# Scores of eight heads, not four, in float32 products straight from the loaded q and k, in the tiles of later heads

## The chip, the cores and the metric

The kernel runs on one core of a Trainium2 chip. The metric is the device time of one execution in microseconds (us). Three runs of the kernel before took 854.75, 860.27 and 860.95 us; their median is 860.27 us. The engines are named as in the profile: PE (TensorE, its matrix products), PEld (its weight loads), DVE (VectorE), ACT (ScalarE), POOL (GpSimd) and SP (SyncE, which here does nothing but issue DMAs).

## What is computed

Three layers follow each other, for 4 batches of 576 tokens: attention with 8 heads of 64 columns and a decay bias from `s`, a gated layer with weights `w_in`, `conv_w` and `w_out`, and a mixer with `U`, `V`, `w_ch1` and `w_ch2`. What the change touches is the product `q k^T` of the first layer.

```python
# attention, for each of 4 x 8 heads (S = 576 tokens, D = 64)
scores = scale * np.matmul(q, k.transpose(0, 1, 3, 2))
cum = np.cumsum(np.maximum(s, 0.0), axis=-1)
bias = -(cum[:, :, :, None] - cum[:, :, None, :])
scores = np.where(causal, -1000000000.0, scores + np.minimum(bias, 0.0))
attn = np.exp(scores - np.max(scores, axis=-1, keepdims=True))
x = np.matmul(attn / (np.sum(attn, axis=-1, keepdims=True) + 1e-09), v)
# gated layer, per token (conv: 3 taps over the tokens)
h = np.maximum(x @ w_in, 0.0)
x = (h * sigmoid(conv(h, conv_w))) @ w_out
# mixer
u = x + ((x.transpose(0, 2, 1)) @ U @ V).transpose(0, 2, 1)
out = u + np.maximum(u @ w_ch1, 0.0) @ w_ch2
```

## The kernel before

**Heads.** The 32 heads (4 batches of 8) are taken one after the other; head h is one call of `att_head(h)` (line 1328), which asks for the loads of head h+1, the scores of head h, and the transposes (`transp`) and the product with v (`av`) of head h-1. The scores of a head are four blocks of 128 queries with 128, 256, 384 and 512 keys (`scores`, tiles `sc`), and a last block of 64 queries with 576 keys, which `scores4` takes for two heads at once in two halves of 288 keys. DVE adds the mask and finds the row's smallest value (line 651), ACT takes the exponential (line 668, into the tiles `P`, or `p4` for the last block), POOL divides by the sum (line 679), PE transposes (line 793, tiles `pt`), ACT copies that out (line 353), and PE multiplies with v (line 829, `av`), which ACT copies into `x` (line 851).

**Two kinds of scores.** The list `FS` (line 28) says which heads take their scores in plain float32 products; before, heads 0 to 3. For such a head `prep4` (line 573) loads q and k of one head from DRAM into the lower 64 partitions of a tile `qkF`, and two rows of the running sum of `s` beside them; one float32 product per block then gives scores and bias. There are two such tiles, for even and for odd heads. For every other head `prep` (line 608) loads q and k of a pair of heads, POOL rounds them to the shorter type fp32r (line 619, "t" from "t" in the profile), DVE subtracts that to get the rest (line 620), and `place` (line 630) copies the parts by DMA, from SBUF to SBUF, into two tiles per head, `tB` (`qkB`) and `tA` (`qkA`), with a small copy of the sum's parts from DRAM (`r_d`). Two fp32r products per block then give the scores. `products` (line 685) issues the one or the two.

**Where the tiles lie.** Before, the `qkF` tiles, the running sum `cc`, its parts `rk` and the mask as loaded (`mraw`) are slices of a large tile `ws`, which later takes weights of the gated layer (`early`, line 411). `qkA` is a ring of two tiles, the tiles t1 and t2 of `prep` are one each, the tile of v for a pair of heads (`vr`) is one.

**Beside the heads.** The weights of the gated layer come as 64-bit numbers, 512 KB a piece, and are taken apart by ACT (line 502), DVE (lines 505 and 515), ACT (353) and POOL (365); `W1_AT` says at which head each piece is asked for, and two raw tiles hold what has landed. When the eight heads of a batch are under way, the gated layer of that batch runs between the next heads' work (`m1_in`, line 893; `m1_out`, line 935); its first steps need `x` of two heads only. The mixer follows after the last head.

**What sets the order.** Each step is handed to `Plan.op` with an engine, an estimate of its duration and what it reads and writes. `Plan.order` then goes through an imagined run: whenever an engine is free there, it takes, of the steps that could start, the one that stands first in the program. The instructions of each engine are issued in the order so found, and on the chip each engine and SP's DMA issues keep to it. A DMA that has to wait (for a tile to come free) holds back all DMAs behind it.

Of the kernel before, what the change touches and what calls it, by code (L numbers as in the profile page):

```python
# [8 lines left out]
F32 = mybir.dt.float32  # L9
F32R = mybir.dt.float32r  # L10
# [8 lines left out]
B, H, S, D = 4, 8, 576, 64  # L19
NH = B * H  # L20
# [4 lines left out]
NF1, NF2 = 8, 16  # L25
KT = DM // 128

FS = range(4)
FV = range(8)

CHUNKS = [512, 512, 512, 512, 256]
# [18 lines left out]
RINGS = dict(P=2, qk=2, th=3, vv=2, qkh=1, x=2, wf=2, xs=5, g=12, hh=3, c=3, x2=4, w64=2, mh=5, o=4, snap=2, tt=4)  # L50
# [259 lines left out]
def tile_attention_moe_mixer(  # L310
# [27 lines left out]
    def dma(nbytes, fn, r, w):  # L338
        return plan.op("SP", 640, fn, r, w, late=nbytes / 360)
# [5 lines left out]
    def pe(ns, fn, r, w):  # L345
        return plan.op("PE", ns, fn, r, w)

    def mm(n, m=128):
        return max(n / 2.4 + 3, m / 1.2)
# [31 lines left out]
    def ring(pool_, cls, count, shape, dtype, name, at={}):  # L381
        n = at[pool_, cls] = at.get((pool_, cls), -1) + 1
        return pool_.buf(f"{cls}{n % count}", shape, dtype, name)
# [15 lines left out]
    ap = Pool(plan, "ap", "right", after=[dec.opened])  # L399

    def one(pool_, name, shape, dtype):
        return pool_.buf(name, shape, dtype, name)
# [8 lines left out]
    def early(name, at, shape, dtype, rows=128):  # L411
        n = 1
        for x in shape:
            n *= x
        axes = " ".join("abc"[: len(shape)])

        def view(t):
            v = t[:rows, at : at + n]
            if dtype != F32:
                v = v.bitcast(dtype)  # L420
            return v.rearrange(f"p ({axes}) -> p {axes}", **dict(zip("abc", shape)))

        return Part(ws, view, name)
# [13 lines left out]
    sm4s = [one(ap, f"sm4_{i}", [128, 5], F32) for i in range(2)]  # L437


    cc = early("cc", 0, (S,), F32, NH)  # L440
    rk = early("rk", 4 * S, (2, S), F32R, NH)
    qkFs = [early(f"qkF_{i}", (6 + 2 * i) * S, (2, S), F32) for i in range(2)]

    def cum():
        return cc()
# [127 lines left out]
    def prep4(h):  # L573

        t = qkFs[h % 2]
        a = slice(64 * (h % 2), 64 * (h % 2) + 64)
        dma(294912, lambda: nc.sync.dma_start(out=t[64:128], in_=qk[h // 2, a]), [], [(t, "q")])
        rows = dma(
            2304, lambda: nc.sync.dma_start(out=t[0:1, 1, :], in_=cum()[h : h + 1]), [cc], [(t, "r0")]
        )  # L580
        if h < 2:
            dma_act(lambda: nc.scalar.dma_start(out=t[1:2, 0, :], in_=cum()[h : h + 1]), [cc], [(t, "r1")])
        else:
            dma(2304, lambda: nc.sync.dma_start(out=t[1:2, 0, :], in_=cum()[h : h + 1]), [cc], [(t, "r1")])
        st.setdefault("first", rows)
        st[h] = dict(qk=[t], P=p_tiles(h), sm=sms[h % 2])

    def prep_v(h):

        vr = ring(ap, "vr", 1, [128, 2, 5, 64], F32, f"vr{h}")  # L590
        dma(327680, lambda: nc.sync.dma_start(out=vr(), in_=vP[h // 2]), [], [vr])
        for o in range(2):
            if h + o in FV:
                st["v", h + o] = (vr, lambda j, o=o: vr[:, o, j, :])
                continue
            vv = ring(ap, "vv", RINGS["vv"], [128, 5, 128], F32R, f"vv{h + o}")
            hi_pool(lambda vv=vv: vv[:, :, 0:64], lambda o=o: vr[:, o], [vr], [(vv, 0)], 320)
            lo_pool(
                lambda vv=vv: vv[:, :, 64:128],
                lambda o=o: vr[:, o],  # L600
                lambda vv=vv: vv[:, :, 0:64],
                [vr, (vv, 0)],
                [(vv, 1)],
                320,
            )
            st["v", h + o] = (vv, lambda j, vv=vv: vv[:, j, :])
# [78 lines left out]
    def products(h, ps, rows, q0, k0, w):  # L685
# [11 lines left out]

        pe(16 + 1.88 * w if h in FS else 2 * mm(w, rows), mms, d["qk"], [ps])

# [606 lines left out]

    prep4(0)
    prep_v(0)
    mraw = early("mraw", 10 * S, (192,), F32)
    dma(98304, lambda: nc.sync.dma_start(out=mraw(), in_=mask_d), [], [mraw])  # L1310
    for c, n in ((0, 384), (512, 224)):
        o = pool(n, lambda c=c, n=n: nc.gpsimd.memset(mask[:, c : c + n], 0.0), [], [(mask, c)], extra=0)
# [15 lines left out]
    def att_head(h):  # L1328

        if h + 1 < NH:  # L1330
            if h % 2 == 1:
                prep_v(h + 1)
            if h + 1 in FS:
                prep4(h + 1)
# [140 lines left out]
    for g in range(2):  # L1475
        blk = (w2a, u1p)[g].buf(f"u{g}", [128, 2 * 7 * S], F32R, f"w2_{g}")
        for i in range(7):
            f = 7 * g + i
# [90 lines left out]
```

## Time and profile before

| | |
|---|---|
| median of three runs | 860.27 us (854.75 to 860.95) |
| the profiled execution | 857.56 us, of which its span 855.7 us |
| PE busy | 813.2 us, 95% of the span |
| PEld, DVE, ACT, POOL busy | 738.0, 610.0, 459.9, 365.3 us |
| DMA | 123.31 MB, 144 GB/s over the span |
| mean granted clock of PE | 0.995 of 2.4 GHz |

A stretch's rows give the busy time of each engine in it; what PE lacks to the stretch's length is PE's idle time. The granted clock is a share of 2.4 GHz: a mean below 1 says that PE ran at 1.2 GHz for a part of the stretch. In the timeline a row is one instruction, or several of one kind that follow each other, with start, duration, the number of them behind an x, and in brackets the idle time ahead of it with what ended that. Products overlap in the pipeline, so the cost of one is read from its start to the start of the next.

### The profile page before, as it was taken

How to read it: one execution, taken by the hardware profiler on the slowest of the kernel's cores; microseconds unless marked ns; L12 is line 12 of the kernel's file. 1: busy time of each engine (PE TensorE's matmuls, PEld its weight loads, DVE VectorE, ACT ScalarE, POOL GpSimd, SP SyncE). 2: the span in 40 equal slices, each digit the busy share in tenths (PEclk: the TensorE clock that was granted, in tenths of full speed). 3: DMA queues.
4: the chain of work that ended last, by engine and by line, in shares of the span. 5: the costliest groups of instructions: out<-in, count | busy, mean ns of one | idle time of the engine just before them, and what ended most of it. 6: DMA issues, size and time to landing. Idle time of an engine off the chain costs nothing. (4 is left out here: it accounts for less than half of the span.)

```text
span 855.7 us, 15636 instructions
## 1 busy us (share of the span) xinstructions
PE 813.2 (95%) x5300; PEld 738.0 (86%) x5300; DVE 610.0 (71%) x1362; ACT 459.9 (54%) x1144; POOL 365.3 (43%) x461
## 2 busy tenths in 40 slices
PE   5889899999999999999999989999999999999998
PEld 2556689889999998998999889999998888888888
DVE  6865899986997769978878998777878762323232
ACT  4776888875987668875766423223233432222211
POOL 4675777574455734457345663333344220000000
PEclk9998999999999999999999999999999999999999
DMA  6868844573455524512133336445467764545443
GB/s 198 234 161 199 202 136 121 141 188 80 122 131 146 129 58 128 149 51 82 34 115 121 118 107 204 145 144 179 138 188 235 256 203 121 163 123 165 130 123 99
DMA packets 67624, 123.31 MB, mean 144 GB/s; under 512 B 9412, under 2 KB 34884, under 8 KB 67544
## 3 DMA queue, kind: packets, MB, share of 16 engines
q1 hardware_dynamic: 67472, 122.30, 50.1%
q8 instruction: 42, 0.69, 0.3%
q14 instruction: 38, 0.31, 0.1%
q10 hardware_dynamic: 72, 0.01, 0.0%
HBM read 68.88 MB, written 28.90 MB: 114 GB/s over the span
## 5 line engine op out<-in xcount | busy, mean ns | idle before, releaser
L1270 PE MATMUL my<-mh,w 128*128 128x512 f32 (+1 forms) x560 | 158.9, 368 | 0.0
L1174 PE MATMUL ma_S<-u,W 128*128 128x288 f32 x768 | 119.2, 296 | 7.6 <-DVE s L1190 7.5
L1251 DVE SCALAR_TENSOR_TENSOR ml<-ml,mh 128x512 fp32r<-128x512 f32 (+1 forms) x80 | 51.9, 654 | 98.3 <-ACT mh L1248 98.3
L935 PE MATMUL y<-gh,w1o 128*128 128x288 f32 x512 | 118.1, 301 | 0.7 <-DVE c L914 0.4
L1270 PEld LDWEIGHTS my<-mh,w 128*128 128x128 f32 x560 | 101.6, 189 | 17.4
L1174 PEld LDWEIGHTS ma_S<-u,W 128*128 128x128 f32 x768 | 107.5, 188 | 10.2 <-DVE s L1190 10.0
L1248 ACT ACTIVATE mh<-ml 128x512 fp32r<-128x512 f32 (+1 forms) x80 | 46.9, 589 | 118.8 <-DMA ml<-ch_d 74.0
L679 POOL TENSOR_SCALAR P<-P,sm 128x128 f32<-128x128 f32 (+3 forms) x128 | 74.9, 602 | 82.2 <-DVE sm L725 61.4
L1270 PE MATMUL my<-ml,w 128*128 128x512 f32 (+1 forms) x280 | 103.0, 368 | 0.0
L1174 PE MATMUL ma_A<-u,W 128*128 128x288 f32 x576 | 92.9, 296 | 0.5 <-DVE s L1190 0.4
L935 PEld LDWEIGHTS y<-gh,w1o 128*128 128x128 f32 x512 | 86.4, 188 | 2.2 <-DVE c L914 1.1
L651 DVE CUSTOM_DVE_ANT_0 sc<-sc,mask 128x128 f32<-128x128 f32 (+2 forms) x144 | 68.8, 494 | 24.3 <-PE sc L690 17.1
L1174 PEld LDWEIGHTS ma_A<-u,W 128*128 128x128 f32 x576 | 81.8, 188 | 1.4 <-DVE s L1190 0.9
L365 POOL TENSOR_TENSOR gl<-c,gh 128x288 fp32r<-128x288 f32 x64 | 53.9, 846 | 64.3 <-ACT gh L920 60.7
L893 PE MATMUL h<-xh,w1h 128*128 128x290 f32 x256 | 80.0, 313 | 0.5 <-DVE c L914 0.5
L893 PE MATMUL h<-xl,w1h 128*128 128x290 f32 x256 | 76.4, 298 | 0.7 <-POOL xl L365 0.7
L893 PE MATMUL h<-xh,w1l 128*128 128x290 f32 x256 | 76.3, 298 | 0.0
L935 PE MATMUL y<-gl,w1o 128*128 128x288 f32 x256 | 75.1, 293 | 0.6 <-POOL gl L365 0.6
L668 ACT ACTIVATE P<-sc,sm 128x128 f32<-128x128 f32 (+3 forms) x128 | 67.5, 530 | 11.2 <-DVE sm L651 9.5
L905 DVE SCALAR_TENSOR_TENSOR c<-h,cw,c 128x288 f32<-128x288 f32 x128 | 64.3, 509 | 5.3 <-ACT c L901 4.3
L1186 ACT COPY p<-ma_A 128x288 f32<-128x288 f32 x64 | 25.5, 399 | 73.0 <-PE ma_A L1174 57.7
L362 DVE TENSOR_TENSOR tl<-pt,th 128x384 fp32r<-128x384 f32 x96 | 54.3, 566 | 12.4 <-ACT th L353 12.1
(145 smaller groups left out, 1990.6 us busy)
## 6 DMA issues: line engine op xcount, KB each, us to landing
ml<-ch_d SPq DMA_DIRECT2D x64, 256.0 KB, 2.6
ch_d<-s SPq DMA_DIRECT2D x64, 144.0 KB, 1.8
raw_w<-w_in SPq DMA_DIRECT2D x16, 512.0 KB
raw_w2a<-w_in SPq DMA_DIRECT2D x16, 512.0 KB, 4.7
raw_w2b<-w_in SPq DMA_DIRECT2D x16, 512.0 KB, 4.4
t<-qk_in SPq DMA_DIRECT2D x28, 288.0 KB, 2.9
qkA<-t SPq DMA_DIRECT2D x56, 144.0 KB, 4.0
qkA<-t SPq DMA_DIRECT2D x28, 288.0 KB, 3.0
```

The source lines that it names most:

```text
L362: dve(n, lambda: nc.vector.tensor_tensor(out(), src(), f32(hi()), ALU.subtract), r, w)
L365: pool(n, lambda: nc.gpsimd.tensor_tensor(out(), src(), f32(hi()), ALU.subtract), r, w, two=True)
L651: lambda: nc.vector.tensor_tensor_reduce(out=ps[:rows, :w], in0=ps[:rows, :w], in1=mask[:rows, m0 : m0 + w], scale=-0.125, scalar=3.0e38 i ...
L668: lambda: nc.scalar.activation(out(), ps[:rows, :w], ACTF.Exp, bias=low(), scale=-1.0, accum_out=total()),
L679: lambda: nc.gpsimd.tensor_scalar(t[:, :w], t[:, :w], r(), 1.0, ALU.mult, ALU.mult),
L893: nc.tensor.matmul(ps[:, :W], lhsT=ww, rhs=xx, start=kt + n == 0, stop=kt == KT - 1 and n == 2)
L905: lambda k=k: nc.vector.scalar_tensor_tensor(c(), hh[:, k : k + HS], cw[:, 3 * f + k : 3 * f + k + 1], c(), ALU.mult, ALU.add),
L935: nc.tensor.matmul(ps[:, :HS], lhsT=ww, rhs=xx(), start=f + n == 0, stop=f == NF1 - 1 and n == 2)
L1174: nc.tensor.matmul(ps[:, :HS], lhsT=ww, rhs=uu, start=k == 0, stop=k == 5)
L1248: act(n, lambda: nc.scalar.activation(mh[:, :n], raw(), ACTF.Relu), [ml], [mh])
L1251: lambda: nc.vector.scalar_tensor_tensor(ml[:, :n], raw(), 0.0, f32(mh[:, :n]), ALU.max, ALU.subtract),
L1270: nc.tensor.matmul(ys[c][dt][:, :n], lhsT=ww, rhs=xx[:, :n], start=f + k == 0, stop=f == NF2 - 1 and k == 2)
```

## The change

`FS` becomes heads 0 to 7. Heads 4 to 7 so take `prep4` and one float32 product per block where they took `prep`, `place` and two fp32r products. The two `qkF` tiles are now the first two of the ring `qkA`, so that the first `place` (heads 8 and 9) waits for the float32 heads to be done with them. The running sum gets a tile of its own, and `rk` and `mraw` move within `ws`.

```diff
-FS = range(4)
+FS = range(8)
...
-    cc = early("cc", 0, (S,), F32, NH)
-    rk = early("rk", 4 * S, (2, S), F32R, NH)
-    qkFs = [early(f"qkF_{i}", (6 + 2 * i) * S, (2, S), F32) for i in range(2)]
+    cc = one(ap, "cc", [NH, S], F32)
+    rk = early("rk", 0, (2, S), F32R, NH)
+    qkFs = [ring(ap, "qkA", RINGS["qk"], [128, 2, S], F32, f"qkF_{i}") for i in range(2)]
...
-    mraw = early("mraw", 10 * S, (192,), F32)
+    mraw = early("mraw", 2 * S, (192,), F32)
```

The planner finds another order for the first part of the program. PE's order is the same again, instruction for instruction, from the last product of head 16 with v on (3103 rows to the end).

SP's issues around the loads for heads 4 and 5, before: `t1`, `t2` hold a pair's parts, lines 638 are the copies of `place`, 525 weights, 618 loads of `prep`, 591 v.

```order
L638 DMA qkA4_291<-t2_4_192 64x576
L638 DMA qkA5_332<-t2_4_192 64x1152
L638 DMA qkB_0_154<-t1_4_200 64x1152
L638 DMA qkB_1_159<-t1_4_200 64x1152
L525 DMA raw_w1_4_0_353<-w1_in 128x512
L638 DMA qkA5_332<-t1_4_200 64x576
L638 DMA qkA5_332<-t2_4_192 64x576
L525 DMA raw_w1_5_0_400<-w1_in 128x512
L618 DMA t1_6_416<-qk_in 128x576
L618 DMA t2_6_423<-qk_in 128x576
L591 DMA vr2_435<-vP_in 128x640
```

And SP's issues at the same place now, where 577, 579 and 584 are the load of q and k and the two rows of `prep4` for head 4:

```order
L525 DMA raw_w1_3_0_305<-w1_in 128x512
L525 DMA raw_w1_4_0_334<-w1_in 128x512
L618 DMA t2_8_361<-qk_in 128x576
L618 DMA t1_8_366<-qk_in 128x576
L638 DMA qkB_0_157<-r_d_57 4x1152
L577 DMA qkF_0_104<-qk_in 64x1152
L579 DMA qkF_0_104<-cc_108 1x16x36
L584 DMA qkF_0_104<-cc_108 1x16x36
L525 DMA raw_w1_5_0_416<-w1_in 128x512
L591 DMA vr2_425<-vP_in 128x640
```

The copies of heads 4 and 5 are gone, one load of q and k stands for them, and the loads of heads 8 and 9 have come forward.

SP's issues ahead of the load of v for heads 4 and 5 (`vr4`), before:

```order
L525 DMA raw_w1_0_512_592<-w1_in 128x512
L638 DMA qkB_0_154<-r_d_57 4x1152
L638 DMA qkB_0_154<-t1_6_416 64x1152
L638 DMA qkA6_626<-t2_6_423 64x1152
L638 DMA qkA6_626<-t1_6_416 64x576
L591 DMA vr4_648<-vP_in 128x640
L638 DMA qkA6_626<-t2_6_423 64x576
```

and now, with head 6's load on `qkF_0`:

```order
L525 DMA raw_w1_7_0_522<-w1_in 128x512
L525 DMA raw_w1_0_512_560<-w1_in 128x512
L577 DMA qkF_0_104<-qk_in 64x1152
L579 DMA qkF_0_104<-cc_108 1x16x36
L584 DMA qkF_0_104<-cc_108 1x16x36
L525 DMA raw_w1_1_512_624<-w1_in 128x512
L591 DMA vr4_631<-vP_in 128x640
```

Around `vr4` the three copies of head 6 have become one load and two rows, and a weight piece stands among them.

PE at the first scores of head 4, before (`pt2` are transposes of head 2, `av2` its product with v):

```order
L793 MATMUL pt2_2_473<-ident_134,P2_2_336 128x128
L690 MATMUL sc4_0_482<-qkB_0_154 128x128
L690 MATMUL sc4_0_482<-qkA4_291 128x128
L690 MATMUL sc4_1_488<-qkB_0_154 128x256
L690 MATMUL sc4_1_488<-qkA4_291 128x256
L829 MATMUL av2_0_491<-tf2_0_451,vr2_435 64x256
```

and now (`h0_0_0` is the gated layer's first block):

```order
L690 MATMUL sc4_0_464<-qkF_0_104 128x128
L793 MATMUL pt2_2_469<-ident_137,p4_1_150 128x128 x2
L793 MATMUL pt2_2_469<-ident_137,P2_3_359 128x128
L793 MATMUL pt2_2_469<-ident_137,P2_2_321 128x128
L690 MATMUL sc4_1_479<-qkF_0_104 128x256
L893 MATMUL h0_0_0_482<-xh0_0_106,w1h_0_241 128x290
L893 MATMUL h0_0_0_482<-xl0_0_110,w1h_0_241 128x290
L893 MATMUL h0_0_0_482<-xh0_0_106,w1l_0_252 128x290
L829 MATMUL av2_0_490<-tf2_0_438,vr2_425 64x256
```

Each pair of products is one, the transposes stand between the two blocks, and one group of three products of the gated layer has come this far forward. In all 24 pairs become single products. Of the gated layer's groups of three, eight stand ahead of head 8's first scores before, and one now; ahead of head 10's first scores it is 16 before and 20 now.

## Rows read from the trace of the kernel before

**Rows 1.** Busy us per stretch: PE, PEld, DVE, ACT, POOL, then clock, DMA share, GB/s.
```profile
17.00:41.00 24.00, 20.82 (x101) 11.90 (x99) 20.12 (x51) 18.80 (x52) 17.64 (x20) 1.00 0.86 224
41.00:55.00 14.00, 13.44 (x75) 9.06 (x74) 12.56 (x37) 12.41 (x35) 9.34 (x13) 1.00 0.44 139
55.00:67.00 12.00, 8.90 (x48) 6.26 (x47) 4.29 (x12) 5.63 (x16) 8.55 (x9) 0.86 0.98 202
67.00:85.00 18.00, 16.00 (x86) 11.47 (x84) 10.82 (x32) 13.16 (x37) 11.37 (x14) 0.91 0.81 206
85.00:110.00 25.00, 21.39 (x134) 17.12 (x134) 22.15 (x61) 19.76 (x54) 17.07 (x22) 1.00 0.81 209
110.00:193.00 83.00, 80.35 (x591) 76.35 (x590) 74.87 (x212) 69.85 (x201) 59.20 (x89) 1.00 0.57 142
```

**Rows 2.** Timeline of PE, its three longest waits between 17 and 85 us.
```profile
38.12 0.52 PE L793 MATMUL pt<-ident,P 128*128 128x128 f32 x3 [1.57 <-ACT x L851]
...
61.45 4.58 PE L829 MATMUL av<-tf,vr 128*64 128x256 f32 x14 [2.34 <-DMA vr<-vP_in]
...
79.28 0.48 PE L793 MATMUL pt<-ident,p 128*128 128x128 f32 x1 [2.00 <-POOL p L679]
```

**Rows 3.** Timeline of PE, float32 scores of heads 2 and 3, each with its successor.
```profile
21.53 0.82 PE L690 MATMUL sc<-ws 128*128 128x128 f32 x4
22.18 0.38 PE L793 MATMUL pt<-ident,p 128*128 128x128 f32 x2
...
32.26 1.38 PE L690 MATMUL sc<-ws 128*128 128x288 f32 x4 [0.26 <-ACT P L668]
33.48 2.22 PE L829 MATMUL av<-tf,vr 128*64 128x320 f32 x10
...
39.75 1.02 PE L690 MATMUL sc<-ws 128*128 128x512 f32 x2
40.61 0.38 PE L793 MATMUL pt<-ident,p 128*128 128x128 f32 x2
```

**Rows 4.** Timeline of PE, fp32r scores of heads 4 and 6, each with its successor.
```profile
46.38 0.40 PE L690 MATMUL sc<-qkB 128*128 128x512 f32 x1
...
46.85 0.49 PE L793 MATMUL pt<-ident,P 128*128 128x128 f32 x3
...
65.96 0.33 PE L690 MATMUL sc<-qkB 128*128 128x128 f32 x1
...
66.52 0.49 PE L793 MATMUL pt<-ident,P 128*128 128x128 f32 x3
...
67.25 0.34 PE L690 MATMUL sc<-qkB 128*128 128x384 f32 x1
...
67.61 0.27 PE L793 MATMUL pt<-ident,p 128*128 128x128 f32 x1
...
71.32 0.32 PE L690 MATMUL sc<-qkB 128*128 128x288 f32 x1
...
71.87 0.29 PE L893 MATMUL h<-xh,w1h 128*128 128x290 f32 x1
```

**Rows 5.** DMA issues from 0 to 110 us: count, KB each, median us to landing.
```profile
qkA<-t SPq DMA_DIRECT2D x16, 144.0 KB, 4.2
...
ws<-qk_in SPq DMA_DIRECT2D x4, 288.0 KB, 4.6
```

**Rows 6.** Timeline of SP, the issue of `vr4`.
```profile
54.48 1.50 SPq L591 DMA_DIRECT2D vr<-vP_in  x1
```

**Rows 7.** Waits of SP's DMA queue from 8 to 110 us: total, times, longest.
```profile
SPq L618 <- DMA qkA<-t: 13.1, 6, 4.9
```

**Rows 8.** Timeline of ACT, the weight piece just ahead of head 1's copy into `x`.
```profile
36.86 0.67 ACT L502 ACTIVATE raw_w<-raw_w 128x512 f32<-128x512 f32 x1 [1.47 <-DMA raw_w<-w_in]
```

**Rows 9.** Timeline of POOL and of DVE, one rounding and one subtraction of `prep`.
```profile
69.35 0.68 POOL L356 TENSOR_SCALAR t<-t 128x576 fp32r<-128x576 f32 x1 [4.48 <-DMA t<-qk_in]
...
72.64 0.74 DVE L362 TENSOR_TENSOR t<-t,t 128x576 fp32r<-128x576 f32 x1
```

## The prediction

> **What bounds the kernel now.** I read the busy times by stretch first, then PE's timeline with its waits, then the timelines and waits of SP and ACT. PE is busy for 95% of the span, and its order is the same again from the last product of head 16 on, which the trace puts near 193 us. What the change is worth is therefore settled before 193 us: what PE gains or loses there is carried to the end, since the work behind is the same, in the same order. Four stretches from 17 to 85 us, the time from head 1 to the first scores of head 8, show PE idle for 3.18, 0.56, 3.10 and 2.00 us [rows 1], 8.8 us together. In two of them the mean granted clock is 0.86 and 0.91. A part f at 1.2 GHz makes the mean 1 - f/2, so work that full speed does in half the time stood for 0.14 x 12 = 1.7 us and 0.09 x 18 = 1.6 us more, 3.3 us together. So 12.1 us are lost there. From 85 to 110 us PE is idle for 3.6 us, from 110 to 193 us for 2.6 us [rows 1]. No other engine is full in these stretches (ACT 18.80 of 24, DVE 20.12 of 24 us), but the DMA engines are busy for 0.81 to 0.98 of three of the four [rows 1]. The reader should see a stage in which many engines wait for each other and DMA is the nearest to full.
>
> The three longest waits tell how [rows 2]. At 38.12 us PE waits 1.57 us for an ACT copy; ACT itself had waited 1.47 us for a weight piece that had not landed [rows 8]. At 61.45 us PE waits 2.34 us for the tile of v of heads 4 and 5; its issue ends at 55.98 us [rows 6], so it took 5.5 us to land among the copies of heads 6 and 7, and the following 14 records took 4.58 us, most of them at 1.2 GHz. At 79.28 us PE waits 2.00 us for POOL's division of the last block.
>
> **What is added.** 24 products in float32 take the place of 48 in fp32r. In float32 the blocks of 128 and 256 keys take 22.18 - 21.53 = 0.65 us together, the one of 512 takes 40.61 - 39.75 = 0.86 us, and two of the four halves of the last block 33.48 - 32.26 = 1.22 us [rows 3]; two halves are one head's share. The block of 384 keys has as many columns as the first two together, so I take 0.65 us. That is 3.38 us a head. In fp32r the same are 66.52 - 65.96 = 0.56, 46.85 - 46.38 = 0.47, 71.87 - 71.32 = 0.55 and, for 384 keys, 67.61 - 67.25 = 0.36 us [rows 4], together 1.94 us. The difference is 1.44 us a head, **+5.8 us** for four heads, 5.4 to 6.5 if each block is off by 0.03 us or so. PE has this work in a stage where it is 85% busy on average, so little of it hides by itself: it counts in full, and only waits that go can pay for it.
>
> **What is removed.** Per head four copies of 288, 288, 144 and 144 KB and one of 18 KB, and for two pairs the loads of 576 KB; added is one load of 288 KB a head with two rows of 2 KB. That is 4.8 MB out and 1.2 MB in, 3.6 MB less. From 17 to 85 us the rates of [rows 1] times the lengths give 13.5 MB, so a quarter of the traffic goes. SP has 12 issues fewer (20 copies and 4 loads out, 12 in), and the loads of `prep` no longer stand behind the copies of heads 4 to 7; such waits held SP's queue for 13.1 us in all from 8 to 110 us [rows 7]. POOL loses four roundings of 0.68 us and DVE four subtractions of 0.74 us [rows 9], 2.7 and 3.0 us. Neither is on PE's path by itself; they shorten queues ahead of it.
>
> Wait by wait. (a) `vr4`: its competitors, the copies of heads 6 and 7, are gone, but a load of 288 KB and a weight piece of 512 KB now stand right ahead of it. PE has, between the last reader of the old v and the first of the new, the scores 5_0 to 5_3 and 6_0 to 6_2 in float32 (2.16 + 1.30 us) and two to three groups of transposes (some 1.3 us before at 0.3 to 0.6 us each, an estimate), about 4.8 us of cover against a landing of 5.5 us with more traffic around it. I take the wait down to 0.5 us and the 1.7 us of clock behind it as gone: **-3.5** (-4.0 to 0). (b) The wait at 38.12 us: the weight piece of [rows 8] now competes with two loads rather than six copies: **-1.0** (-1.6 to 0). (c) The wait at 79.28 us rests on DVE, ACT and POOL in turn and on two weight pieces that ACT meets ahead of the last block's exponentials in the new order as well; two of DVE's subtractions stood in that chain. I leave it and its clock as they are: **0** (-3.6 to +2). (d) The rest of the idle time to 85 us is 8.8 - 5.9 = 2.9 us in short waits; a quarter less traffic and the shorter queues of POOL and DVE take a third: **-1.0** (-2 to +1). (e) Seven groups of three products of the gated layer come later than before and are there to fill PE between heads 8 and 10, where it is idle for 3.6 us: **-1.3** (-2.5 to +1).
>
> **What is new.** Heads 4 to 7 now wait, as heads 2 and 3 did, until the head two before is done with the tile. Then come three issues and a landing of 4.6 us [rows 5]. For head 4 there is much room: its tile is free when the last block of head 2 is done at 33.5 us [rows 3], and its scores start after 40 us. For head 6 the cover is the same work as in (a), about as long as the load; behind the waiting load SP holds a weight piece and `vr4`. For head 8 three copies, each 4.2 us to landing [rows 5], wait for head 6's last block, with a like cover. I take 0.3 us for each: **+0.6** (0 to +4: one of them late by 2.3 us as `vr4` was, with 1.7 us of clock). The moved tiles cost nothing else: `cc`, `rk` and `mraw` are read by the same steps as before, and the first use of `ws` by weights comes later than their last.
>
> The sum is 5.8 - 3.5 - 1.0 - 1.0 - 1.3 + 0.6 = -0.4 us, on the profiled execution's 857.6 us: 857.2 us. The median of the three runs lies 2.7 us above that execution, so the same change on it gives **859.9 us**.
>
> The clock is the least certain term. Rows show it fall around the wait of 2.34 us and in the stretch with the wait of 2.00 us, and not in the stretch with the one of 1.57 us [rows 1, 2]. The Trainium skill, TensorE: Matmul & The Clock Gate, section "What's actually happening", has the chip judge activity in windows that run free of the kernel, so that the same wait may or may not cost the clock from one kernel to the next; by that the 3.3 us could come back with shorter waits, and the sum would be 1.7 us higher, or 1.6 us lower if the second drop goes by luck. The trace neither bears this out nor speaks against it.
>
> **The rivals.** First, DMA was the real bound up to 85 us, and with a quarter of it gone PE runs through: nearly all of the 12.1 us go, and half of the 3.6 us behind. Then 5.8 - 12.1 - 1.8 = -8.1 us, 852.2 us on the median. For it speaks the DMA share of 0.81 to 0.98; against it that the wait at 79 us hangs on POOL, and that weights still come at the pace at which ACT and DVE free the raw tiles.
>
> Second, the slower one: PE's waits stay because weight pieces, not copies, are what ACT and DVE stand behind. ACT takes a piece apart ahead of the last block's exponentials of heads 4 and 6; a piece that lands late holds the exponentials, POOL's division and PE's transposes. Then nothing of (a) to (e) comes back, and the time is +5.8 us, 866.1 us on the median; with one more wait like that of `vr4`, 2.3 + 1.7 us, it is 870 us. It decides when the pieces of 512 KB land later than the about 5 us that PE's work covers.
>
> Third, the added products fall into time in which PE would wait anyway, since ACT and DVE set the pace, while copies and roundings were hidden as well. Then the price is a part of 5.8 us and the gain a part of (a): within 2 us of no change, 858 to 862 us.
>
> **How the numbers follow.** The forecast, -4 to +3 us, has a chance of 0.50; the third rival, which ends in the same place, 0.17; the first 0.13; the second 0.20. One per cent is 8.6 us, about what a measurement of this kernel can tell from no change. Faster by over 1% needs more than the first rival's 8.1 us: half of its chance, 0.06. Slower by over 1% needs the second rival with its further wait: 0.08. Within 1%: 0.86. The range reaches from the first rival's 852.2 to the second's 866.1 us, rounded outwards to 852 and 867; the likeliest case's own range is 856 to 863 us.
>
> **What would show it.** Right: the 24 float32 products of heads 4 to 7 cost what those of heads 2 and 3 did; `vr4` lands within 5 us and PE waits under 1 us for it; the clock in the stretch around it stays at 1.00; PE's idle time to head 8's first scores falls to 4 to 6 us; the last product of head 16 with v ends within 4 us of where it did, and the time from there to the end is the same. Wrong: waits of 2 us or more at head 6's or head 8's first scores, or at the transposes of the last blocks, with a fall of the clock behind them; or no waits at all there.

## Result, and the profile after

In the runs beside each other the changed kernel took 849.47 us (848.97 to 850.11), the kernel before 858.89 us; the ratio is 0.990 with a 95% interval of 0.988 to 0.992. A second set on another chip gave 850.40 us, 0.991 (0.989 to 0.993). The forecast was 859.9 us with a range of 852 to 867: the time lies 10.4 us under the forecast and below the range. Of that, 1.4 us is the kernel before itself, which stands at 858.89 us here and stood at 860.27 us when the forecast was made.

The profiled execution has a span of 847.6 us for 855.7 us, 8.1 us less. First the windows of after by stretch, the columns as in [rows 1]; the last two cut the time at head 8's first scores and at head 16's last product with v.

```profile
17.00:41.00 24.00, 22.36 (x109) 13.31 (x109) 20.00 (x55) 20.20 (x56) 19.44 (x20) 1.00 0.61 189
41.00:55.00 14.00, 13.46 (x62) 7.70 (x63) 11.32 (x25) 10.48 (x28) 8.23 (x11) 1.00 0.69 171
55.00:67.00 12.00, 10.43 (x52) 6.03 (x51) 9.78 (x26) 9.14 (x26) 8.23 (x9) 1.00 0.54 167
67.00:85.00 18.00, 16.74 (x87) 10.48 (x86) 11.45 (x37) 14.74 (x42) 11.73 (x16) 1.00 0.70 186
85.00:110.00 25.00, 24.74 (x177) 22.73 (x176) 24.14 (x65) 22.78 (x63) 20.58 (x26) 1.00 0.60 165
...
17.00:77.30 60.30, 55.30 (x261) 32.08 (x260) 49.41 (x126) 48.12 (x131) 42.84 (x47) 1.00 0.60 173
77.30:185.54 108.24, 105.92 (x770) 98.81 (x768) 95.28 (x272) 91.08 (x260) 75.65 (x114) 1.00 0.62 157
```

The kernel before, cut at the same two places of its program:

```profile
17.00:84.49 67.49, 58.65 (x299) 38.18 (x297) 47.79 (x128) 49.48 (x137) 46.80 (x54) 0.95 0.78 198
84.49:193.17 108.68, 102.42 (x729) 94.15 (x728) 97.20 (x273) 90.12 (x256) 76.37 (x111) 1.00 0.63 157
```

Three things are to be seen. PE's idle time from 17 us to head 8's first scores fell from 8.84 to 5.00 us. The clock is 1.00 there, where 0.95 over 67.49 us stood for 3.4 us. And behind that point the same part of the program takes the same time (108.24 for 108.68 us), with 3.9 us less idle time and 3.5 us more work: seven groups of the gated layer that stood ahead of head 8 now stand behind it. Their 21 products make some 3 us of that, at 0.13 to 0.14 us each from start to start (before's timeline):

```profile
87.20 0.30 PE L893 MATMUL h<-xh,w1h 128*128 128x290 f32 x1
87.33 0.30 PE L893 MATMUL h<-xl,w1h 128*128 128x290 f32 x1
```

So 7.2 of the 8.1 us are won before head 8's first scores (84.49 to 77.30 us). From head 16's last product to the end it is 662.1 us, before 662.5.

The clock is a large part of the gain, and not in these two executions alone. Over all executions on record the granted clock, averaged over the span, has a mean of 0.992 to 0.993 in the kernel before (by chip) and of 0.998 to 0.999 in the kernel after; on 858 us that is some 4 to 6 us, an estimate.

PE's timeline after, at the waits that answer to [rows 2]:

```profile
37.70 0.30 PE L793 MATMUL pt<-ident,p 128*128 128x128 f32 x1 [1.40 <-ACT P L668]
...
58.00 0.33 PE L793 MATMUL pt<-ident,p 128*128 128x128 f32 x1 [1.57 <-POOL p L679]
...
60.49 0.86 PE L829 MATMUL av<-tf,vr 128*64 128x256 f32 x4
...
76.77 0.33 PE L793 MATMUL pt<-ident,p 128*128 128x128 f32 x1 [0.31 <-POOL p L679]
...
77.30 0.31 PE L690 MATMUL sc<-qkB 128*128 128x128 f32 x1
```

The wait for `vr4` (2.34 us) is gone: the row at 60.49 us has no bracket. The wait at the last block ahead of head 8 is 0.31 us for 2.00. Two waits of 1.4 and 1.6 us are left, on ACT's exponentials and on POOL's division. SP's timeline and its waits show the load's place:

```profile
53.68 0.37 SPq L591 DMA_DIRECT2D vr<-vP_in  x1
```

```profile
SPq L618 <- DMA qkA<-t: 3.2, 3, 1.5
```

The issue took 0.37 us for 1.50 [rows 6] and began 0.8 us earlier, and the loads of `prep` stood 3.2 us behind copies for 13.1 [rows 7].

### The profile page after: what moved, and what is told of

The parts are those of the page before. It is cut to its first block, busy times and chain, and to the rows that moved or that the text cites. A ratio compares the mean times of both kernels' runs of the same rounds, so it can differ in the third digit from the quotient of the medians.

```text
span 847.6 us, 15572 instructions
## 1 busy us (share of the span) xinstructions
PE 812.5 (96%) x5300; PEld 736.3 (87%) x5300; DVE 608.0 (72%) x1358; ACT 460.3 (54%) x1144; POOL 363.0 (43%) x457
```

## The experiments

All ratios are to the kernel before on the same chip. Since the program behind head 8's first scores takes 107.9 to 109.9 us to head 16's last product in every kernel with after's order, the time of head 8's first scores tells what a change of the first part costs; "idle" is PE's from 17 us to there, "clock" the mean there. These three columns come from one profiled execution each: after and c1, the same kernel, differ by 0.2 us at head 8's first scores and by 0.7 us at head 16's last product. The medians hold more than the first part: the profiled executions of c1, e2, e3, e5 and e9 have one or two falls of the clock between 400 and 500 us, where PE's order is after's, those of after, e1, e4 and e10 none.

| kernel | median, us | ratio, 95% interval | head 8's first scores | idle | clock |
|---|---|---|---|---|---|
| before (profile above) | 858.89 | | 84.49 | 8.84 | 0.95 |
| after | 849.47 | 0.990 (0.988 to 0.992) | 77.30 | 5.00 | 1.00 |
| after again (c1) | 850.40 | 0.991 (0.989 to 0.993) | 77.06 | 5.05 | 1.00 |
| e1: copies back | 857.18 | 0.998 (0.997 to 0.999) | 83.81 | 10.26 | 0.97 |
| e2: roundings back | 852.71 | 0.992 (0.991 to 0.994) | 78.85 | 7.00 | 1.00 |
| e3: both back | 859.96 | 1.001 (1.000 to 1.003) | 86.22 | 10.54 | 0.93 |
| e4: cheap products | 850.02 | 0.989 (0.988 to 0.991) | 78.43 | 10.48 | 0.97 |
| e5: copies of 4 KB | 856.61 | 0.997 (0.994 to 0.999) | 81.16 | 7.20 | 0.97 |
| e9: 8 copies ahead of `vr4` | 854.56 | 0.996 (0.994 to 0.998) | 81.53 | 7.43 | 0.95 |
| e10: 8 copies behind it | 851.99 | 0.993 (0.991 to 0.996) | 78.78 | 7.33 | 1.00 |

**What was removed, put back: e1, e2, e3.** The kernel after gets copies like those of heads 4 to 7 back with no reader (e1; two of 288 and two of 128 KB a head, without the small copies from `r_d` and the loads of `prep`), the four roundings and four subtractions (e2), or both (e3). The order of PE, ACT and of the rest of DVE's steps stays that of after.

```diff
+    def extra(h):
+        if not 4 <= h < 8:
+            return
+        after = st[2]["pe", 0, 0] if h < 6 else st[4]["pe", 512, 288]
+        for n in range(4):
+            t = xd[4 * (h % 2) + n]
+            r, w = (128, S) if n < 2 else (64, 512)
+            o = plan.op("SP", 0, lambda t=t, r=r, w=w: nc.sync.dma_start(out=flat(t)[:r, :w], in_=flat(xsrc)[:r, :w]), [xsrc], [t])
+            o.preds.add(after)
...
+        st[h] = dict(qk=[t], P=p_tiles(h), sm=sms[h % 2])
+        extra(h)
```

> The kernel after, with copies of the same sizes as those of heads 4 to 7 issued by SP at about the places that they had (four a head, 288, 288, 128 and 128 KB, from a filled tile into tiles that are not in use yet); nothing reads them, and the order of PE, DVE and ACT is that of the kernel after. If the traffic of the copies made the waits and the falls of the clock before (theory one), this costs 6 to 9 us: 855 to 859 us, with waits of 1.5 us or more for v or for a weight piece and a clock under 1 in the stretch from 45 to 85 us. If the roundings on POOL and DVE made them (theory two), or the order of the instructions (theory three), it stays within 1.5 us of the 849.5 us of the kernel after.

> The kernel after, with four roundings of 128x576 on POOL and four subtractions on DVE put back at about the places that those of heads 4 to 7 had, on tiles that nothing reads; no DMA is added. Theory one (traffic of the copies) and theory three (order): 849 to 851 us. Theory two (queues of POOL and DVE): 853 us or more, with longer waits of PE for the division of the last blocks.

> The kernel after with the copies and the roundings put back together, in the order of the kernel after, and with its float32 products. Theories one and two: what the two single runs cost adds up, 855 to 862 us. Theory three (the order of the kernel after has fewer waits whatever else runs): 852 us or less.

e1 gives back 7.7 us, e2 3.2 us, e3 10.5 us: put back in this way, copies and roundings cost 10.5 us, nearly the sum of the parts, and e3, which has both beside after's float32 products and in after's order, is as slow as before. PE's timeline in e1, and in e3:

```profile
66.88 0.83 PE L849 MATMUL av<-tf,vr 128*64 128x256 f32 x4 [3.57 <-DMA vr<-vP_in]
```

```profile
32.55 0.33 PE L813 MATMUL pt<-ident,p 128*128 128x128 f32 x1 [3.74 <-ACT P L688]
...
68.27 1.51 PE L849 MATMUL av<-tf,vr 128*64 128x256 f32 x4 [3.66 <-DMA vr<-vP_in]
```

With the copies the wait for `vr4` is there again, larger than before. One reason is their place: before has three copies and a small one ahead of `vr4`, e1 a block of all eight, and a weight piece (SP's timeline in e1):

```profile
55.86 5.40 SPq L582 DMA_DIRECT2D xd<-xsrc  x8
...
61.99 0.38 SPq L611 DMA_DIRECT2D vr<-vP_in  x1
```

So the 7.7 and 10.5 us are the price of copies in blocks of eight; no run measures it at before's places.

With the roundings alone (e2) there is no wait for `vr4`; PE's waits from 8 to 200 us (total, times, longest), in e2 and then in after, tell what they did:

```profile
PE pt L813 <- ACT P L688: 4.0, 4, 1.3
PE pt L813 <- POOL p L699: 1.3, 2, 1.0
PE av L849 <- ACT tf L353: 0.7, 1, 0.7
```

```profile
PE pt L793 <- ACT P L668: 2.6, 3, 1.4
PE pt L793 <- POOL p L679: 1.9, 2, 1.6
```

PE waits 1.4 us longer for exponentials and 0.7 us for one of ACT's copies ahead of a product with v, and not longer for POOL's division. Together it is 2.0 us more idle time to head 8's first scores, with no single long wait and no fall of the clock up to there.

**What was added, taken out: e4.** Heads 4 to 7 take two bf16 products per block, on the upper halves of the numbers in the same tiles and in after's order; their scores are coarser.

```diff
-            for c, t in enumerate(d["qk"]):
+            two = 4 <= h < 8
+            ts = [t().bitcast(BF16).rearrange("p a (n two) -> p a n two", two=2)[:, :, :, 1] for t in d["qk"]] * 2 if two else d["qk"]
+            for c, t in enumerate(ts):
```

> The kernel after, where heads 4 to 7 take two products of one pass per block (on the upper halves of the same float32 numbers, so the scores are coarser) in place of one float32 product: PE has the product time of the kernel before there, in the order of the kernel after. If the float32 products count in full, as the prediction had it, this gives 849.5 - 5.8 = 843.7 us; if they lie in time in which PE would wait anyway, 848 to 850 us; in between, the part that counts is read off.

The time stays (850.02 for 849.47 us). The windows of e4 to head 8's first scores, and its waits from 8 to 200 us:

```profile
17.00:78.43 61.43, 50.95 (x262) 30.31 (x261) 49.00 (x127) 48.60 (x133) 42.72 (x47) 0.97 0.62 172
```

```profile
PE pt L795 <- POOL p L679: 3.4, 2, 2.3
PE pt L795 <- ACT P L668: 2.5, 2, 1.3
PE sc L692 <- ACT p L668: 1.8, 5, 0.7
```

PE is busy for 50.95 us, 4.35 us less than in after, and with the clock at 0.97 (1.8 us of the 61.43) about 6 us less work is done. The idle time grew by 5.5 us. So the added product time is as large as forecast, and nearly all of it lies in time in which PE would wait for POOL and ACT: taking it out buys nothing. The low clock has a part in this: it follows the wait of 2.3 us for POOL's division, and without its 1.8 us head 8's first scores would come at some 76.6 us, 0.7 us ahead of after's. And the order was held: a planner that knew of the shorter products might have put other work there.

**Twelve heads: e7.** `FS` becomes heads 0 to 11, for the stretch where PE is fuller.

```diff
-FS = range(8)
+FS = range(12)
```

> The kernel after with twelve heads in float32 products rather than eight. Heads 8 to 11 run where PE is busy for 97 to 99% in the kernel after. If float32 products are free only where PE waits anyway, four heads more cost up to 4 x 1.44 = 5.8 us less a little for their copies: 851 to 856 us. If the copies and roundings are dear everywhere, another 3 us or more are gained: 846 us or less.

```profile
PE 821.8 (96%) x5300; PEld 738.9 (87%) x5300; DVE 606.8 (71%) x1354; ACT 460.7 (54%) x1144; POOL 357.7 (42%) x453
```

854.59 us, 0.996 (0.994 to 0.999) of before, 5.1 us above after and 4.2 us above c1. PE's busy time on the page is 9.3 us above after's 812.5; with the mean clock of 0.996 (3.4 us of 854.0) that leaves 5.9 us for four heads' products. The low clock lies far behind them, between 400 and 500 us, so what they cost is read up to head 16's last product with v, which starts at 189.53 us in e7. Windows of e7, and of after to the same product:

```profile
17.00:189.53 172.53, 167.76 (x1024) 130.51 (x1023) 141.52 (x392) 139.71 (x388) 114.31 (x156) 1.00 0.51 137
400.00:500.00 100.00, 91.80 (x648) 88.98 (x647) 83.58 (x145) 55.53 (x124) 51.66 (x45) 0.97 0.27 91
```

```profile
17.00:185.54 168.54, 161.22 (x1027) 130.90 (x1026) 144.69 (x397) 139.21 (x390) 118.49 (x160) 1.00 0.61 163
```

At a clock of 1.00 in both, PE has 6.5 us more work and 2.6 us less idle time, and comes there 4.0 us later. The same price that cost nothing in heads 4 to 7 is mostly paid in heads 8 to 11, although copies and roundings went there as well. The planner's order is another one, so the split is not exact.

**Half of the change: e6, e8, e11.** e6 gives the kernel before a second tile of v; e8 gives it eight float32 heads and leaves the tiles where they were; e11 moves the tiles and leaves four float32 heads.

```diff
-        vr = ring(ap, "vr", 1, [128, 2, 5, 64], F32, f"vr{h}")
+        vr = ring(ap, "vr", 2, [128, 2, 5, 64], F32, f"vr{h}")
```

> The kernel before with two tiles for v, so that the load for heads 4 and 5 need not wait for heads 2 and 3 and lands early. If the wait of 2.3 us for it and the fall of the clock behind it cost what they show, this gives 859 - 4 = 855 us, with the clock at 1.00 in the stretch from 55 to 67 us. If the stage is held up by everything that shares the DMA engines, another wait takes its place: 858 us or more.

> The kernel before with eight heads in FS and nothing else: the float32 tiles stay in the tile that takes the second half of the gated layer's weights, which so has to wait until head 7's scores are done, some 25 us later than in the kernel after. If the move of the tiles matters, this loses a good part of the gain: 853 to 860 us, with raw weight tiles held and waits of ACT or PE between 50 and 110 us. If it does not: 849 to 851 us.

> The kernel after with four float32 heads, not eight: the tiles lie where the change puts them, the rest of the work is that of the kernel before, and the planner orders it anew. Theory 'the gain needs both halves of the change' (e8, the eight heads without the move of the tiles, came out at 1.003 of the kernel before): copies and roundings of heads 4 to 7 stand ahead of the load of v again, so 855 to 860 us, 0.996 to 1.002 of the kernel before. Rival 'the place of the tiles is what brings it': 849 to 852 us.

e6: 860.24 us, 1.003 (1.000 to 1.005). The wait for v is gone and another stands at the place of the first of [rows 2], larger; ACT had waited 3.78 us for a weight piece there:

```profile
39.73 0.59 PE L793 MATMUL pt<-ident,P 128*128 128x128 f32 x3 [3.90 <-ACT x L851]
```

e8: 861.29 us, 1.003 (1.001 to 1.006). Head 8's first scores come at 79.19 us, 5.3 us before the kernel before's; head 16's last product ends at 195.21 us, 2 us after it. The planner finds another order behind head 8, with the loads bunched (windows of e8, columns as in [rows 1]):

```profile
100.00:110.00 10.00, 7.45 (x46) 6.00 (x45) 7.06 (x17) 6.94 (x18) 7.52 (x12) 0.98 0.90 252
110.00:120.00 10.00, 10.00 (x69) 9.98 (x68) 8.99 (x26) 8.65 (x27) 5.18 (x8) 0.85 0.15 33
```

PE idles 2.6 us while DMA is at 0.90, and a stretch at the low clock follows. What in the old layout makes the planner choose so is not known. e11: 855.75 us, 0.998 (0.996 to 1.000); no long wait for v is left there, and POOL's divisions are waited for instead (6.6 us in seven waits from 8 to 200 us). Head 8's first scores come at 81.58 us, 2.9 us before the kernel before's, with the clock at 1.00 to there, and that is lost again behind them.

e11 says one thing more. It has the copies and roundings of heads 4 to 7, and its expectation was that they stand ahead of `vr4` again. They do not: in the planner's new order SP issues it behind one copy and the small one of head 6, and PE waits at most 0.3 us for a load of v.

```profile
52.67 0.35 SPq L591 DMA_DIRECT2D vr<-vP_in  x1
```

So a wait for `vr4` does not follow from the copies being there; where they stand in SP's queue decides with it. As to the two halves: each alone wins ahead of head 8's first scores, loses it behind and leaves the time within 0.4% of before. That only both together keep the gain is shown; why is not, since the planner's order differs in each.

**Queue or bytes: e5, c1, e9, e10.** e5 is e1 with copies of 4 KB, as many and at the same places in SP's queue. e9 puts back only the eight copies of heads 6 and 7, ahead of `vr4`; e10 puts the same eight behind it. c1 is after, once more.

```diff
-            r, w = (128, S) if n < 2 else (64, 512)
+            r, w = 16, 64
```

```diff
-        if not 4 <= h < 8:
+        if not 6 <= h < 8:
...
+        vrd = dma(327680, lambda: nc.sync.dma_start(out=vr(), in_=vP[h // 2]), [], [vr])
+        if h == 4:
+            extra(6, vrd)
+            extra(7, vrd)
```

The first hunk of the second diff alone is e9; e10 has the other lines, and `after` is then `vrd`.

> As e1_copies, with the same 16 issues by SP at the same places, but each copies 4 KB only (16 rows of 256 bytes). If the copies cost by the bytes that they put on the DMA engines, this is within 1.5 us of the kernel after: 848.5 to 851 us. If they cost by SP's time (issues, and loads queued behind them), it is near e1_copies: 854 to 858 us.

> The kernel after, once more, as the measure for the three runs beside it on the same chip. Earlier it stood at 0.990 of the kernel before; if the chip makes no difference, 0.988 to 0.992 here.

> The kernel after with eight copies of no use put back (the four of head 6 and of head 7, two of 288 KB and two of 128 KB each), issued by SP just ahead of the load of heads 4 and 5's v; TensorE, ScalarE and VectorE keep their order. Theory 'the order of the queue': the eight issues take SP 5.4 us (as in e1, 55.86 to 61.26), the load of v is issued some 6 us later and TensorE waits for it again, 2.5 to 3.5 us, with a stretch at the low clock behind it: +4 to +7 us on the kernel after. Theory 'what counts is the bytes': the 1.66 MB take some 6 to 9 us of the sixteen DMA engines wherever they stand, so this run and e10_behind8 cost alike.

> The same eight copies with the same bytes as in e9_ahead8, issued by SP behind the load of v and behind head 7's q and k (58.24 us in the kernel after), where SP has nothing to issue until 64.39 us. Theory 'the order of the queue': the eight issues of 0.67 us fit this gap, nothing is late, 0 to +1 us on the kernel after. Theory 'the bytes': the load of v is still under way (issued 53.68, used from 60.5) and the next two weight pieces are fetched beside 1.66 MB more, so a wait of 1 us or more comes back and it costs like e9_ahead8.

SP's timeline in e5, e9 and e10, in this order:

```profile
53.98 5.33 SPq L582 DMA_DIRECT2D xd<-xsrc  x8
...
60.03 0.38 SPq L611 DMA_DIRECT2D vr<-vP_in  x1
```

```profile
52.26 5.12 SPq L582 DMA_DIRECT2D xd<-xsrc  x8
...
58.18 0.57 SPq L611 DMA_DIRECT2D vr<-vP_in  x1
```

```profile
52.71 0.37 SPq L610 DMA_DIRECT2D vr<-vP_in  x1
...
57.31 6.19 SPq L582 DMA_DIRECT2D xd<-xsrc  x8
```

And PE's, in e5 and in e9, where v is first used (in e10 that row has no wait):

```profile
64.10 1.41 PE L849 MATMUL av<-tf,vr 128*64 128x256 f32 x4 [2.67 <-DMA vr<-vP_in]
```

```profile
63.22 1.51 PE L849 MATMUL av<-tf,vr 128*64 128x256 f32 x4 [3.50 <-DMA vr<-vP_in]
```

Eight issues of 4 KB take SP 5.33 us, eight of 288 and 128 KB 5.12 us: an issue of these copies costs SP some 0.65 us whatever it moves. Of e1's 6.5 us at head 8's first scores the tiny copies alone bring 3.9, of its 6.7 us at head 16's last product 5.1 (192.26 and 190.61 for 185.54 us), so SP's time is the larger part. By the medians e5 is as slow as e1, but its profiled execution loses 3.4 us at the low clock between 400 and 500 us. Whether the bytes cost something of their own is less sure. e10 was expected to cost nothing or up to 1 us by the theory of the queue. Against c1 it cost 1.6 us on the median, with intervals that overlap; in the profiled executions, of which e10's is the fastest of its six, it is 1.7 us at head 8's first scores and 0.9 us at head 16's last product (187.08 for 186.21 us). Its idle time, 7.33 us, is that of e9. What sets e9 apart is the clock, 0.95 over 64.53 us or 3.2 us, as the idle time stands in one wait of 3.50 us; in e10 it is spread over waits up to 1.8 us. The DMA engines are full in e10 from 55 to 67 us:

```profile
55.00:67.00 12.00, 10.54 (x55) 6.33 (x54) 8.67 (x26) 10.30 (x29) 5.78 (x8) 1.00 1.02 265
```

So the theory of the queue holds: the issues make `vr4` late and cost the clock behind its wait. That the bytes make everything else on the DMA engines a little late fits e10's idle time, but its cost of about 1 us is within what executions of one kernel differ by.

The Trainium skill, DMA: Bandwidth & Descriptors, section "Issuing engines are not separate DMA queues", calls the time that the sequencer takes to start a DMA usually small relative to the DMA itself. For one it is, here some 0.65 us against the 4.2 us to landing of before's copies [rows 5]; for eight in a row, 5.33 us in e5, it is not.

## Why the prediction was wrong, point by point

**The frame held.** The order of PE from head 16's last product on is unchanged and so is the time from there (662.1 for 662.5 us). Everything is decided ahead of it, as the prediction said. Of its signs of being right, PE's idle time of 4 to 6 us to head 8's first scores (5.00), the short wait for `vr4` (none) and the clock at 1.00 came true; the one that weighs the whole sum did not, since head 16's last product came 7.6 us earlier and not within 4.

Up to that product the sum can be laid beside the trace. PE's work, with the low clock taken out, rose by 3.5 us where +5.8 was entered. Idle time and low clock up to head 8's first scores fell by 7.2 us where (a) to (d) and the new waits made -4.9. Idle time behind them fell by 3.9 us where (e) had -1.3. That is -7.6 us for -0.4.

**The step that failed first: "it counts in full, and only waits that go can pay for it".** The size of +5.8 us was right: e7's busy time gives 5.9 us for four heads, e4's about 6. But e4 shows its price in time as nothing (+0.5 us without it, within the intervals). The prediction weighed the work against PE's mean share of 85% in the stage (it is 87% up to head 8's first scores, 58.65 of 67.49 us) and took idle time as something that other terms would remove; it did not ask whether the added products stand where PE waits for ACT, DVE and POOL. They do. The wait at 79.28 us, which step (c) left at 0, shows it: in after that row waits 0.31 us, e4 with the shorter products 1.13 us at the same place. The longer products ahead of it fill the time in which POOL gets to its division. The other half of it is the planner's: with eight float32 heads seven groups of the gated layer (21 products of some 0.14 us, 2.9 us) moved from ahead of head 8 to behind it, into idle time. It is the heads that do this and not the tiles: e8, with the old layout, has one group ahead of head 8 as well, e11, with four float32 heads, eleven. Step (e) saw the move, and gave it 1.3 us; the idle time there fell by 3.9 us (6.26 to 2.32 us). The move and the added products come from one change, and the prediction entered the cost in full and the return at a third.

**What was removed was sized too low.** Steps (a) to (d) and the new waits made -4.9 us for the 7.2 us that went; that copies and roundings can hold PE up by as much e3 shows, with 10.5 us. (a) was right: -3.5 forecast for `vr4` and its clock, the wait is gone and the clock back. (b) was wrong in kind: the wait at 38.12 us became one of 1.40 us at 37.70 us on the exponentials; nearly nothing was won. (c), forecast 0 with its bounds at -3.6 and +2, came out near the lower bound: the wait fell by 1.7 us and the stretch's clock went from 0.91 to 1.00. (d) held roundings, subtractions and traffic at 1.0 us together; e2 measures 3.2 us for the eight instructions. The prediction said "Neither is on PE's path by itself", and they are not on it as one long wait, but they make its short ones longer.

**New waits** of heads 4, 6 and 8 for their tiles: +0.6 us forecast, none seen. The first scores of heads 4, 6 and 8 have no wait; those of head 6 (58.60 us) follow closely on the wait of 1.57 us for POOL, which would hide a tile that came somewhat late.

**The rivals.** The third had the products right (they fall into time in which PE would wait) and the copies wrong (they were not hidden). The first had the total right, -8.1 us as in the profiled executions (852.2 us for 849.47 on the medians), but partly by luck: it let 13.9 us of waits and low clock go and paid 5.8 us for the products, where 11.1 us went and work rose by 3.5 us. Its mechanism, the DMA engines' time, is not what the runs show most of: e5, e9 and e11 point to where issues stand in SP's queue, and to the clock behind a wait. The truth takes its price from the third and most of its gain from the first, a pair that the prediction did not put together. The slower rival, weight pieces as the real hold, is refuted by the result: the pieces are the same and the waits went. In e6 a late piece does hold PE, for 3.90 us.

**What stays open.** PE's work rose by 3.5 us and not by 5.8, over the whole page by 3.6 (812.5 us, before 813.2 less 4.3 us for the low clock). Some 2 us of PE's busy time in before have no cause here; by lines they lie in the products with v (829), whose busy time to head 16's last product falls from 51.0 to 46.2 us, more than the low clock explains. What the copies cost at before's own places, and why the gain needs both halves of the change, is not measured. And e5 and e7 ran on a chip on which the kernel before spread from 854 to 863 us, so the differences of their medians to after are good to about 2 us.

## What to carry to other kernels

Here work added to an engine that was 87% busy was free, because it stood ahead of that engine's waits for others; look at each wait behind the added work and ask what would have been done in that time, before it is entered into a sum. Take cost and return of one event from the same place: when added work moves filler work into later idle time, the two can cancel. Before copies are weighed by their bytes, count the issues that stand ahead of a load that the bottleneck waits for: here copies of 4 KB held that load as long as copies of 288 KB.

## What the runs showed of the hardware

The clock went with where PE's idle time lies, not with how much there is. e9 and e10 have nearly the same idle time to head 8 (7.43 and 7.33 us); stretches of 3 us in e9, and in e10, columns as in [rows 1]:

```profile
61.00:64.00 3.00, 0.78 (x2) 0.52 (x3) 0.93 (x2) 0.67 (x1) 1.94 (x4) 0.79 0.93 337
64.00:67.00 3.00, 3.00 (x9) 1.49 (x8) 0.88 (x2) 1.71 (x5) 0.00 (x0) 0.50 0.60 160
67.00:70.00 3.00, 3.00 (x11) 1.70 (x10) 2.64 (x3) 0.93 (x3) 1.78 (x1) 0.58 0.19 74
```

```profile
67.00:70.00 3.00, 2.17 (x9) 0.84 (x9) 0.76 (x4) 0.86 (x4) 0.99 (x5) 1.00 0.66 243
70.00:73.00 3.00, 2.07 (x10) 1.22 (x10) 2.31 (x3) 1.57 (x3) 3.00 (x4) 1.00 0.90 188
```

In e9 PE is busy for 0.78 of the 3 us from 61 to 64 us and runs at 1.2 GHz from 64 to 67 us, all of it, although it is busy throughout; in e10 PE is idle for 0.83 and 0.93 us in two neighbouring stretches and stays at 2.4 GHz. The executions taken together go the same way: the clock over the span has a mean of 0.994 in e9's twelve (0.990 to 0.998) and of 0.998 in e10's six (0.996 to 1.000). The spread says too that one kernel, in one order, loses the clock more often in one execution than in another. A single long wait is not needed, though, as e11 shows (columns PE busy, clock, DMA share and GB/s):

```profile
88.00:91.00 3.00, 1.84 (x9) 1.00 0.50 141
91.00:94.00 3.00, 1.85 (x10) 1.00 0.65 144
94.00:97.00 3.00, 1.65 (x9) 0.78 0.97 257
97.00:100.00 3.00, 3.00 (x13) 0.50 0.79 260
```

The longest wait there is 1.45 us, but PE was idle for over a third of three stretches in a row, and the fall came in the third. The Trainium skill, TensorE: Matmul & The Clock Gate, section "HAM oscillation — how this bites in real kernels", tells of products too short to cover the wait for the next load and of a clock that falls at each such wait; e9 agrees for its one late load, and e11, which waits for POOL and ACT, shows that no load has to be late.

An issue of one of the copies put back took SP 0.67 us for 4 KB and 0.64 us for 288 and 128 KB (5.33 and 5.12 us for eight; 6.19 us in e10, with the DMA engines full), so a row of small copies was as long a hold for the load behind it as a row of large ones. Other loads took other times: in after 0.37 us for the 320 KB of `vr4`, where the same load took 1.50 us in before [rows 6].
